# First MLP product: the last pair's P5 with hi beside lo weights, its upper half added through DRAM, and the helper jobs of two stages re-timed

## The chip, the cores and the metric

The kernel runs on one core of one Trainium2 chip. The metric is the device time in microseconds of one execution, the median of several runs. A profiled execution has, beside its time, a span: from its first to its last recorded instruction. Five engines matter: PE (TensorE, with its weight loads as a row of their own, PEld), DVE (VectorE), ACT (ScalarE), POOL (GpSimd, which here issues all accumulating DMAs and a few memsets) and SP (which issues the loads).

## The reference

The input x has 2048 tokens of 640 channels (S, D below), the MLP has 1728 hidden units (F). All is float32.

```python
xn = layernorm(x)                      # no affine part
h  = layernorm(xn)
a  = xn @ dft_hid_re.T ;  b = xn @ dft_hid_im.T
y1 = dft_seq_re @ a - dft_seq_im @ b   # FNet mixing, real part
u  = gelu(h.T @ w1 + b1)               # (D, F): the token-mixing MLP, gelu with tanh
y2 = (u @ w2 + b2).T                   # (S, D)
out = x + y1 + y2
```

## The kernel before

**Number format.** PE takes float32r operands. Each operand is cut into a high part (`high`, an ACT copy to float32r, line 138) and a low part (`low`, a DVE subtraction, line 141). A product is then three matmuls (`three`, lines 149, 150 and 152): high weights by high moving, high weights by low moving, low weights by high moving. The weights are the matrices from DRAM (the "pieces", 128 rows by 512 or 640 columns, cut into blocks of 128), the moving operands are 320 columns of data that stay in SBUF (tiles `shid`, `sup`, `sdown`).

**Stages.** First the products with `dft_seq` (lines 477 and 595, until about 405 us of the span), then four stages of rows: `hid` (8 units, products with `dft_hid`), `up0` and `up1` (7 units each: the first MLP product over the first and the second half of the tokens), `down0` and `down1` (8 units each: the second MLP product over two parts of the hidden units). A unit handles a pair of output row blocks by a Winograd form of Strassen's scheme, with seven products P1, P5, P6, P2, P7, P3, P4 in this order. Each product is a step of the list `steps`; in `up0` and `up1` a step has 4 blocks of 3 matmuls of 128x320.

**The last pair.** The hidden units fill 13 blocks of 128 and a tail of 64 (`TAIL`). Block 13 is paired with block 6 in the last unit, r = 6, of `up0` and of `up1`; on the host its 64 columns are laid out twice. Before the change, the steps P7 and P4 of that unit, whose weights come from block 13 alone, are cut so that the 64 columns of high parts stand beside 64 columns of low parts in one block of weights (`cut_piece` with `tail`, lines 183 to 193): two matmuls per block do, not three. The result has the product with high weights in partitions 0 to 63 of the bank, which DVE adds (line 836), and that with low weights in partitions 64 to 127, which cannot be added across partitions: ACT copies it to a spare tile (line 945) and POOL adds it to the unit's partial result in DRAM by an accumulating DMA (line 934). In `up0` these DMAs wait until the unit's whole result is stored (`end`, line 907), since they add to it.

**Order of the work.** It is written by hand. Turn i (`turn_of`) emits, in this order: `loads[i]` (SP), `reads[i]` (the results of step i-1 out of their PSUM bank, by ACT line 854 or DVE line 841), `sums[i]` (DVE sums of the raw weights, lines 785 and 144), the high cut of step i+2 (ACT), `extras[i]`, `timed[i]`, helper jobs, the low cut of step i+2 (DVE), `behind_lo[i]`, and the matmuls of step i. Every engine takes its instructions in that order. P1, P6, P7 and P4 of a unit accumulate in one PSUM bank (`z`), P5 and P3 in another (`y`), P2 has its own, so that P6, for example, cannot start before ACT has read P1 out of the bank that they share; in the last unit P7 and P4 have a bank `v`.

**Jobs.** The moving operands of the next stage are made by jobs out of a list, at most one per turn: `get` (a load), two normalizations on ACT, and `job0` to `job5` of `moving_of`, of which `job1`, `job2`, `job3` and `job5` are DVE work and are stored as tuples. A turn is "short" when its index is not in `LONG_AT`; a short turn leaves a tuple at the head of the list for later. `None` entries take a turn each.

**Gelu.** In `up1`, unit r's result is gathered by a POOL DMA that adds the part from DRAM (line 911), and two turns of `gelu` (line 916) follow some 14 turns after the unit's start. The first of them is preceded by the load of ACT's table for gelu.

Of the kernel before, what the change touches and what calls it, by code (L numbers as in the profile page):

```python
# [11 lines left out]
AF = mybir.ActivationFunctionType  # L12
ALU = mybir.AluOpType

P = 128
# [6 lines left out]
TAIL = F - NF * P  # L22
# [5 lines left out]
H2 = D // 2  # L28
# [33 lines left out]


LONG_AT = (
    ((0, 1, 3, 6), 7), ((0, 1, 3, 6, 7, 8, 10, 14, 15, 17, 20), 21), ((0, 1, 3, 6), 7), ((0, 1, 3), 7),
)


# [1 line left out]
def fnet_plus_mixer(  # L70
# [30 lines left out]
    nc = tc.nc  # L101
# [8 lines left out]
    one = keep.tile([P, 1], F32, name="one")  # L110
# [32 lines left out]
    def sub(to, a, b):  # L143
        nc.vector.tensor_sub(to, a, b)  # L144
# [19 lines left out]
    steps = []  # L164
    loads, sums, reads, extras, timed, behind_lo = (defaultdict(list) for _ in range(6))
# [103 lines left out]
    def part_of(tag, n):  # L269
# [7 lines left out]
    place = {  # L277
        "v": lambda: pair_at("v"), "ca": lambda: pair_at("ca"), "cb": lambda: pair_at("cb"),
        "x0": part_of("xb", 0), "x1": part_of("xb", 1), "x2": part_of("xb", 2),
    }  # L280
# [486 lines left out]
    def row_steps(stage, nq, load_piece, at, end, bias=(None, None), base=None, earliest=0, each=None, aside={}, tail=False, stacked=()):  # L767

        s0, n = len(steps), nq * P
        raw, banks, held = {}, {}, {}

        def load(*names):
            for name in names:
                raw[name] = raw_slot(n)
                load_piece(raw[name], int(name[1]) - 1, int(name[2]) - 1)  # L780

        def first_sum():
            k = n if n == D else CH
            raw["s"] = raws[k][:, raws[k].shape[1] - 1, :n]
            nc.vector.tensor_add(raw["s"], raw["A21"], raw["A22"])  # L785
            if stacked:

                at = slice(n - P, n)
                nc.vector.tensor_copy(raw["s"][TAIL:, at], raw["A21"][TAIL:, at])

        order = (1, 5, 6, 2, 7, 3, 4)

        early = n < D
        loads_of = {-6: ("A11", "A21", "A22"), -4: ("A12",)} if early else {
            -5: ("A11",), -4: ("A21", "A22"), -1: ("A12",),
        }
        operand = {1: "A11", 5: "s", 6: "A11", 2: "A12", 7: "A21", 3: "A12", 4: "A22"}

        sums_of = {
            -2: (first_sum, lambda: sub(raw["A21"], raw["A11"], raw["A21"])),  # L800
            -1: (lambda: sub(raw["A11"], raw["s"], raw["A11"]),),
            2: (lambda: sub(raw["A12"], raw["A12"], raw["A11"]),),
        }
        bank_of = {1: "z", 6: "z", 7: "z", 4: "z", 5: "y", 3: "y", 2: "w"}
        new_bank = (1, 5, 2)
        if tail:
            bank_of.update({7: "v", 4: "v"})
            new_bank += (7,)
        of_moving = {1: 0, 2: 1, 3: 2, 5: 3, 7: 4, 4: 5, 6: 6}

        goes_to = {1: (0, 0, True), 5: (1, 1, True), 6: (0, 1, True), 2: (0, 0, False), 7: (1, 1, False),
                   3: (0, 1, False), 4: (1, 0, True)}

        def products(i):
            def run(w):
                if i in new_bank:
                    banks[bank_of[i]] = bank()
                for q in range(nq):
                    ks = slice(q * P, (q + 1) * P)
                    m = moving[stage, q]  # L820
                    three(
                        banks[bank_of[i]][:, :H2],
                        (w[0][:, ks], None if w[1] is None or i in stacked and q == nq - 1 else w[1][:, ks]),
                        (m[:, 0, of_moving[i], :], m[:, 1, of_moving[i], :]), i in new_bank and q == 0, q == nq - 1,
                    )
            return run

        def read(i):
            def run():
                if i == 1:  # L830
                    held["c"] = place[at]()
                row, half, fresh = goes_to[i]
                cols = slice(half * H2, (half + 1) * H2)
                c, b = held["c"][:, row, cols], banks[bank_of[i]][:, :H2]
                if tail and i in (7, 4):
                    nc.vector.tensor_add(c[:TAIL], b[:TAIL], c[:TAIL])
                    aside[i](row, half, b)
                elif i in aside:
                    aside[i](row, half, b)
                elif not fresh:  # L840
                    nc.vector.tensor_add(c, b, c)
                elif base and i == 4:

                    for k, queue in enumerate((nc.sync, nc.scalar)):
                        of = slice(k * H2 // 2, (k + 1) * H2 // 2)
                        nc.vector.tensor_add(c[:, of], b[:, of], base()[:, row, cols][:, of])
                        each(c, row, half, True, of, queue)
                    return
                elif base:
                    nc.vector.tensor_add(c, b, base()[:, row, cols])  # L850
                elif bias[row] is not None:
                    nc.scalar.activation(c, b, AF.Identity, bias=bias[row])  # L852
                else:
                    nc.scalar.activation(c, b, AF.Copy)  # L854
                if tail and i == 6:

                    low_row = held["c"][:, 1, :]
                    nc.vector.tensor_add(low_row[:, H2:], b, low_row[:, H2:])
                    nc.scalar.activation(low_row[:, :H2], b, AF.Copy)
                if each:  # L860
                    each(c, row, half, i in (2, 7, 3, 4))
                elif i == 4:
                    end(held["c"])
            return run

        for e, names in loads_of.items():
            loads[max(s0 + e, earliest)].append(lambda names=names: load(*names))
        if s0 == s_hid:


            operand[6] = "s"
            behind_lo[s0 - 2].append(first_sum)
            sums_of = {
                0: (lambda: sub(raw["s"], raw["s"], raw["A11"]),),
                1: (lambda: sub(raw["A21"], raw["A11"], raw["A21"]),),
                2: (lambda: sub(raw["A12"], raw["A12"], raw["s"]),),
            }
        for e, fs in sums_of.items():
            sums[s0 + e].extend(fs)
        for e, i in enumerate(order):  # L880
            steps.append(cut_piece(lambda i=i: raw[operand[i]], n, tail and i in (7, 4), i in stacked) + (products(i),))
            reads[s0 + e + 1].append(read(i))
        return s0

# [13 lines left out]
    def up(stage, r, at):  # L898
# [3 lines left out]
        tail = r == NF2 - 1  # L902
        halves = []
# [29 lines left out]
        def add_to(t, rows, row, half):  # L933
            nc.gpsimd.dma_start(part_up[r][rows, row, half * H2 : (half + 1) * H2], t, accum_op=ALU.add)

        def by_dram(i):
            def run(row, half, b):

                t = place["x1"]()[:, (r + (i == 4)) % 2, i // 7 * H2 : (i // 7 + 1) * H2]
                if not (tail and i in (7, 4)):  # L940
                    nc.scalar.activation(t, b, AF.Copy)
                    add_to(t, slice(P), row, half)
                    return
                t = t[P - TAIL :]
                nc.scalar.activation(t, b[P - TAIL :], AF.Copy)
                if stage == 0:
                    halves.append((row, half, t))
                else:
                    add_to(t, slice(TAIL), row, half)
            return run  # L950

        aside = (2, 7) if stage else ()
        if tail:
            aside += (7, 4)
        s0 = row_steps(
            f"up{stage}", 4, load_piece, at, end, earliest=s_up - 4, aside={i: by_dram(i) for i in aside}, tail=tail,
        )
# [59 lines left out]
    for q in range(4):  # L1017
        get, changes, rest = rows_again(0, q, "v")
# [4 lines left out]
    for r in range(NF2):  # L1023
        up(0, r, ("ca", "cb")[r % 2])
    gets, changes, rests = zip(*(rows_again(1, q, ("v", "x0")[q % 2]) for q in range(4)))
    timed[s_up - 6].append(lambda: jobs.extend([gets[0], None, None] + changes[0]))
    timed[s_up + 2].append(lambda: jobs.extend(
        [gets[1]] + rests[0] + [gets[2]] + changes[1] + rests[1] + [gets[3]] + changes[2] + rests[2]
        + changes[3] + rests[3]
    ))  # L1030
    for r in range(NF2):
        up(1, r, ("x2", "ca", "cb", "v", "x0")[r % 5])
    s_down = len(steps)
# [12 lines left out]
    def do_jobs(n, short=False):  # L1046

        while n > 0 and jobs and not (short and isinstance(jobs[0], tuple)):
            f = jobs.pop(0)
            n -= 1  # L1050
            if f:
                (f[0] if isinstance(f, tuple) else f)()
# [25 lines left out]
    with tc.manual_schedule():  # L1078
        for word in START.split():
            start[word[0]](*map(int, word[1:].split("-")))  # L1080
        for i in range(8, len(steps) + 1):
# [5 lines left out]
            elif i >= s_hid:  # L1087
                k = sum(i >= s for s in (s_up, s_up + 7 * NF2, s_down))
                at, of = LONG_AT[k]
# [43 lines left out]
```

## Time and profile before

| | |
|---|---|
| runs | 876.32, 875.50, 875.51 us: median 875.51 |
| profiled execution | 875.92 us, of which its span 874.2 us |
| PE busy | 869.0 us (99% of the span), 4924 matmuls |
| PE weight loads busy | 793.1 us (91%) |
| DVE busy | 711.7 us (81%) |
| ACT busy | 530.2 us (61%) |
| POOL busy | 126.2 us (14%) |
| granted TensorE clock | 0.999 |
| stage `up0` | 528.9 to 614.3 us of the span |
| stage `up1` | 614.3 to 700.0 us |

Matmuls overlap in the profile, so that the busy time of PE says little on its own: what a matmul costs is the distance from one start to the next, and what is lost is seen where that distance grows. The weight loads stand in a row of their own (PEld), and there the waits show.

### The profile page before, as it was taken

To read this page: it belongs to the slowest core of one execution; us is meant where nothing else is said; L and a number is where in the kernel's file an instruction comes from. 1 tells how busy PE (TensorE), PEld (TensorE's weight loads), DVE (VectorE), ACT (ScalarE), POOL (GpSimd) and SP (SyncE) were. 2 spreads that over 40 slices of the span, in tenths; PEclk is the share of its full clock that TensorE was granted. 3 is DMA by queue.
4 is the path that set the end of the run, shared out by engine and by line. 5 is a ranking of instruction groups with operands and counts; after the bars stand their busy time and mean duration, and the time that the engine had idled before them with its cause. 6 is when DMAs were issued, how large, how long until landed. Compare 5 with 4: busy or idle time off the path is not lost.

```text
span 874.2 us, 13999 instructions
## 1 busy us (share of the span) xinstructions
PE 869.0 (99%) x4924; PEld 793.1 (91%) x4924; DVE 711.7 (81%) x1217; ACT 530.2 (61%) x960; POOL 126.2 (14%) x170
## 2 busy tenths in 40 slices
PE   9999999999999999999999999999999999999998
PEld 6888888888888888889999999999999999999998
DVE  7878878795887978788887787998678978897887
ACT  5746576764556566557565556675577766555553
POOL 0110100101121111222010101000212221111211
PEclk9999999999999999999999999999999999999999
DMA  7771554619385556869666756454678797766786
GB/s 270 231 266 76 194 203 132 242 59 357 54 219 92 163 119 133 208 92 195 168 127 166 156 139 196 162 177 138 142 170 181 169 244 193 190 136 133 151 173 139
DMA packets 86087, 147.64 MB, mean 169 GB/s; under 512 B 8512, under 2 KB 35904, under 8 KB 85760
## 3 DMA queue, kind: packets, MB, share of 16 engines
q1 hardware_dynamic: 64928, 95.80, 34.0%
q0 software_dynamic: 20800, 50.70, 30.6%
q8 instruction: 38, 0.62, 0.3%
q14 instruction: 33, 0.27, 0.1%
q10 hardware_dynamic: 288, 0.25, 0.1%
HBM read 99.96 MB, written 52.00 MB: 174 GB/s over the span
## 4 chain that ended last, share of the span: by engine, by line
PE 94%; DVE 3%; ACT 1%; DMA 1%; issue 1%; DVEq 0%; ACTq 0%
PE psum L149 30%; PE psum L150 30%; PE psum L152 29%; PE psum L477 5%; DVE piece L141 1%; DMA pieces<-y 1%; DVE pieces L144 0%; DMA x<-in_x 0%; ACT piece L138 0%; ACT n L259 0%; ACT x L259 0%; DVE pair L144 0%; DVE st L210 0%; DVE pieces L785 0%; DVE shid L141 0%
## 5 line engine op out<-in xcount | busy, mean ns | idle before, releaser
L141 DVE TENSOR_TENSOR piece<-pieces,piece 128x512 fp32r<-128x512 f32 (+2 forms) x524 | 350.1, 671 | 125.8 <-ACT piece L138 119.1
L138 ACT ACTIVATE piece<-pieces 128x512 fp32r<-128x512 f32 (+3 forms) x508 | 318.1, 627 | 212.0 <-PE psum L152 143.5
L150 PE MATMUL psum<-piece,n 128*128 128x512 f32 x504 | 196.4, 390 | 0.0
L149 PE MATMUL psum<-piece,n 128*128 128x512 f32 x504 | 196.2, 389 | 0.0
L152 PE MATMUL psum<-piece,n 128*128 128x512 f32 x504 | 196.1, 389 | 0.0
L149 PE MATMUL psum<-sup,piece 128*128 128x320 f32 x392 | 121.2, 310 | 0.0
L149 PE MATMUL psum<-sdown,piece 128*128 128x320 f32 x392 | 121.0, 309 | 0.0
L150 PE MATMUL psum<-sup,piece 128*128 128x320 f32 x392 | 120.9, 309 | 0.0
L150 PE MATMUL psum<-sdown,piece 128*128 128x320 f32 x392 | 120.9, 309 | 0.0
L152 PE MATMUL psum<-sup,piece 128*128 128x320 f32 x376 | 116.6, 310 | 0.0
L152 PE MATMUL psum<-sdown,piece 128*128 128x320 f32 x376 | 116.2, 309 | 0.0
L144 DVE TENSOR_TENSOR pieces<-pieces 128x512 f32<-128x512 f32 (+3 forms) x142 | 112.7, 794 | 2.6
L150 PEld LDWEIGHTS psum<-piece,n 128*128 128x128 f32 x504 | 94.6, 188 | 21.0 <-DVE piece L141 1.5
L149 PEld LDWEIGHTS psum<-piece,n 128*128 128x128 f32 x504 | 94.6, 188 | 19.9
L152 PEld LDWEIGHTS psum<-piece,n 128*128 128x128 f32 x504 | 94.6, 188 | 19.3
L152 PE MATMUL psum<-shid,piece 128*128 128x320 f32 x280 | 86.6, 309 | 0.1
L150 PE MATMUL psum<-shid,piece 128*128 128x320 f32 x280 | 86.5, 309 | 0.0
L149 PE MATMUL psum<-shid,piece 128*128 128x320 f32 x280 | 86.5, 309 | 0.0
L854 ACT ACTIVATE pair<-psum 128x320 f32<-128x320 f32 x102 | 44.5, 436 | 54.6 <-PE psum L152 49.8
L149 PEld LDWEIGHTS psum<-sup,piece 128*128 128x128 f32 x392 | 73.6, 188 | 0.6 <-ACT pairs L854 0.3
L149 PEld LDWEIGHTS psum<-sdown,piece 128*128 128x128 f32 x392 | 73.6, 188 | 0.2 <-ACT pair L852 0.2
L150 PEld LDWEIGHTS psum<-sup,piece 128*128 128x128 f32 x392 | 73.6, 188 | 0.0
(106 smaller groups left out, 1115.8 us busy)
## 6 DMA issues: line engine op xcount, KB each, us to landing
pieces<-in_dft_seq SPq DMA_DIRECT2D x128, 256.0 KB, 5.4
pieces<-in_w SPq DMA_DIRECT2D x88, 256.0 KB, 3.7
y<-c POOLq DMA_DIRECT2D x84, 256.0 KB, 6.1
out<-pair POOLq DMA_DIRECT2D x38, 320.0 KB, 5.3
pieces<-y SPq DMA_DIRECT2D x32, 320.0 KB, 3.9
pieces<-in_w SPq DMA_DIRECT2D x32, 192.0 KB, 3.1
out<-in_x SPq DMA_DIRECT2D x16, 320.0 KB, 7.1
up<-pair POOLq DMA_DIRECT2D x8, 640.0 KB, 3.2
```

Of the source, the lines that this page charges most:

```text
L138: nc.scalar.activation(hi, src, AF.Copy)
L141: nc.vector.tensor_sub(lo, src, hi.bitcast(F32))
L144: nc.vector.tensor_sub(to, a, b)
L149: nc.tensor.matmul(psum, wh, mh, start=first, stop=False, skip_group_check=True)
L150: nc.tensor.matmul(psum, wh, ml, start=False, stop=last and wl is None, skip_group_check=True)
L152: nc.tensor.matmul(psum, wl, mh, start=False, stop=last, skip_group_check=True)
L477: nc.tensor.matmul(banks[m, j], channels(k, j)[rows], w[cols], start=n == 0 and k == begin, stop=n == 2 and k == end, skip_group_check=True,)
L854: nc.scalar.activation(c, b, AF.Copy)
```

## The change

- **P5 of the last pair** (r = 6, in `up0` and `up1`) is cut like P7 and P4. Its operand is the sum A21 + A22. `first_sum` now adds only the first 64 columns of each block and sets the other 64 to zero, which the two sums made from it need (one shorter DVE addition and one memset for one full addition). The step has two matmuls per block, not three.
- **P5 gets a bank of its own** ("u"), since its upper half is not to be accumulated into: five banks for that unit, not four, which shifts the turn of the banks behind it. P3 starts the bank "y".
- **C12** (row 0, right half) takes P5's lower partitions straight from bank u by a DVE addition of 64x320 (`behind_lo` of turn s0+4, a new instruction). P5's upper half is copied by ACT and added by two DMAs, to C22 and to C12 (a new ACT copy of 64x320, two new POOL DMAs of 80 KB in each of the two stages).
- **Order in the last pair**: the ACT copies of the upper halves, and the store of the unit after P4, move from `reads` to `extras`, that is behind the high cut of the same turn; so does ACT's copy of C21 (line 859 before). In `up0`, P7's upper half stands first among the DMAs that follow the store, then P5's two, then P4's.
- **Jobs**: in `hid` the turn of index 6 becomes short; in `up0` long turns are now 0, 1 and 3 of every seven (before: 0, 1, 3, 6, 7, 8, 10, 14, 15, 17, 20 of every 21); three `get` entries no longer take a turn of their own.
- **Gelu table**: a small activation of a one-column tile with gelu stands in turn 7 of `up1`, so that the table is loaded there.

On the engines: 8 matmuls with their weight loads fewer (4 in each tail unit), 4 more DVE instructions, 3 more on ACT, 4 more DMAs on POOL; on SP one pair of loads of x stands one load of y later.

```diff
 LONG_AT = (
-    ((0, 1, 3, 6), 7), ((0, 1, 3, 6, 7, 8, 10, 14, 15, 17, 20), 21), ((0, 1, 3, 6), 7), ((0, 1, 3), 7),
+    (tuple(i for i in range(56) if i % 7 in (0, 1, 3, 6) and i != 6), 56), ((0, 1, 3), 7), ((0, 1, 3, 6), 7),
+    ((0, 1, 3), 7),
 )
...
+            if tail:
+                s1, a21, a22 = (raw[a].rearrange("p (q c) -> p q c", c=P) for a in ("s", "A21", "A22"))
+                nc.vector.tensor_add(s1[:, :, :TAIL], a21[:, :, :TAIL], a22[:, :, :TAIL])
+                nc.vector.memset(s1[:, :, TAIL:], 0.0)
+                return
             nc.vector.tensor_add(raw["s"], raw["A21"], raw["A22"])
...
         if tail:
-            bank_of.update({7: "v", 4: "v"})
-            new_bank += (7,)
+            bank_of.update({5: "u", 7: "v", 4: "v"})
+            new_bank += (7, 3)
...
-                if tail and i in (7, 4):
-                    nc.vector.tensor_add(c[:TAIL], b[:TAIL], c[:TAIL])
-                    aside[i](row, half, b)
-                elif i in aside:
+                if tail and i in (5, 7, 4):
+
+                    def upper():
+                        aside[i](row, half, b)
+                        if i == 4:
+                            end(held["c"])
+
+                    extras[s0 + order.index(i) + 1].append(upper)
+                    if i == 5:
+                        nc.scalar.activation(c, b, AF.Copy)
+                    else:
+                        nc.vector.tensor_add(c[:TAIL], b[:TAIL], c[:TAIL])
+                    return
+                if i in aside:
...
-                    nc.scalar.activation(low_row[:, :H2], b, AF.Copy)
+                    extras[s0 + 3].append(lambda: nc.scalar.activation(low_row[:, :H2], b, AF.Copy))
+                    p5 = banks["u"][:TAIL, :H2]
+                    behind_lo[s0 + 4].append(lambda: nc.vector.tensor_add(c[:TAIL], p5, c[:TAIL]))
...
-            steps.append(cut_piece(lambda i=i: raw[operand[i]], n, tail and i in (7, 4), i in stacked) + (products(i),))
+            steps.append(cut_piece(lambda i=i: raw[operand[i]], n, tail and i in (5, 7, 4), i in stacked) + (products(i),))
...
+                for k in (0, 1) if i == 5 else (row,):
+                    if stage == 0:
+                        halves.insert(0 if i == 7 else len(halves), (k, half, t))
+                    else:
+                        add_to(t, slice(TAIL), k, half)
...
-            aside += (7, 4)
+            aside += (5, 7, 4)
...
-        [gets[1]] + rests[0] + [gets[2]] + changes[1] + rests[1] + [gets[3]] + changes[2] + rests[2]
+        [[gets[1]]] + rests[0] + [[gets[2]]] + changes[1] + rests[1] + [[gets[3]]] + changes[2] + rests[2]
...
+    extras[len(steps) + 7].append(lambda: nc.scalar.activation(one, one, AF.Gelu_apprx_tanh))
...
+            if isinstance(f, list):
+                f[0]()
+                continue
```

More of the change, by code (lines that the diff above doesn't have):

```diff
@@ L937, in run @@
             def run(row, half, b):
-                t = place["x1"]()[:, (r + (i == 4)) % 2, i // 7 * H2 : (i // 7 + 1) * H2]
-                if not (tail and i in (7, 4)):
+                at = i in (5, 7)
+                t = place["x1"]()[:, (r + (i in (5, 4))) % 2, at * H2 : (at + 1) * H2]
+                if not (tail and i in (5, 7, 4)):
                     nc.scalar.activation(t, b, AF.Copy)
@@ L945, in run @@
                 nc.scalar.activation(t, b[P - TAIL :], AF.Copy)
[L946 to L949, printed above, removed]
+                for k in (0, 1) if i == 5 else (row,):
[3 more added lines that the diff above has]
+                        add_to(t, slice(TAIL), k, half)
             return run
```

## The prediction

> **What bounds the kernel.** I read the page first, then the waits of the weight loads, then the order of time of single engines around each wait.
>
> ```profile
> PE 869.0 (99%) x4924; PEld 793.1 (91%) x4924; DVE 711.7 (81%) x1217; ACT 530.2 (61%) x960; POOL 126.2 (14%) x170
> ```
> ```profile
> PEld psum L150 <- DVE piece L141: 1.5, 8, 0.3
> ...
> PEld psum L152 <- DVE piece L141: 0.3, 1, 0.3
> PEld psum L149 <- ACT pairs L854: 0.3, 1, 0.3
> PEld psum L149 <- ACT pair L854: 0.3, 1, 0.3
> PEld psum L149 <- ACT pair L852: 0.2, 1, 0.2
> ```
> PE is the bound, and it hardly ever waits: single waits of 0.2 to 0.3 us. So the change can win the pace of the matmuls that it drops and these few waits, and nothing else. The pace is the distance of starts:
>
> ```profile
> 569.83 0.31 PE L152 MATMUL psum<-sup,piece 128*128 128x320 f32 x1
> ...
> 570.42 0.31 PE L149 MATMUL psum<-sup,piece 128*128 128x320 f32 x1
> ```
> Four starts in 0.59 us: 0.147 us for one matmul, not the 0.31 us that its row shows.
>
> **Dropped matmuls.** Four blocks in P5 of each last unit lose one: 4 x 0.147 = 0.59 us in `up0` and 0.59 us in `up1`, 1.17 us together. That is all that PE itself gains; it holds only if the other engines bring everything 0.59 us earlier.
>
> **The job moved in `hid`.**
> ```profile
> 423.48 0.19 PEld L152 LDWEIGHTS psum<-shid,piece 128*128 128x128 f32 x1 [0.34 <-DVE piece L141]
> ```
> ```profile
> 421.35 0.49 DVE L141 TENSOR_TENSOR sup<-pair,sup 128x320 fp32r<-128x320 f32 x1
> 421.87 0.83 DVE L144 TENSOR_TENSOR pair<-pair 128x640 f32<-128x640 f32 x1
> 422.61 0.82 DVE L141 TENSOR_TENSOR piece<-pieces,piece 128x640 fp32r<-128x640 f32 x1
> ```
> PE waits 0.34 us for the low cut at 422.61, ahead of which DVE does a `job1` (421.35 to 422.61, 1.26 us). The short turn 6 moves that job behind the cut, which then is 1.26 us earlier: -0.34. Next late would be the following cut, but that one has the same work ahead of it as before. Later jobs slide by up to three turns and meet again at turn 24. SP's pair of x loads one place later is costed at nothing: its normalization keeps three turns of distance.
>
> **Jobs in `up0`.** Twice a low cut comes late there, in the units r = 1 and 4:
> ```profile
> 543.26 0.38 PE L152 MATMUL psum<-sup,piece 128*128 128x320 f32 x1
> 543.48 0.31 PE L149 MATMUL psum<-sup,piece 128*128 128x320 f32 x1
> ...
> 545.09 0.41 PE L152 MATMUL psum<-sup,piece 128*128 128x320 f32 x1
> 545.34 0.31 PE L149 MATMUL psum<-sup,piece 128*128 128x320 f32 x1
> ```
> Distances 0.22 and 0.25, 0.17 over the pace; r = 4 shows the same form once more, which I count alike: 0.34 in all. Both have a DVE job in turn 6 of a unit, right behind turn 5 with its two sums. With long turns 0, 1 and 3 alone no DVE job stands in turns 4 to 6: -0.34. What was done earlier now lies later: `job1`, `job2` and `job3` of the fourth row come to turns 0, 1 and 3 of the last unit, `job5` to turn 0 of `up1`.
>
> **The last unit of `up0`.** This is where I expect the loss. Before:
> ```profile
> 608.64 0.44 ACT L854 ACTIVATE pair<-psum 128x320 f32<-128x320 f32 x1 [1.01 <-PE psum L152]
> ```
> ```profile
> 609.11 0.49 DVE L858 TENSOR_TENSOR pair<-psum,pair 128x320 f32<-128x320 f32 x1 [1.03 <-ACT pair L854]
> 610.63 0.69 DVE L141 TENSOR_TENSOR piece<-pieces,piece 128x512 fp32r<-128x512 f32 x1 [1.02 <-ACT piece L138]
> 611.24 0.48 DVE L841 TENSOR_TENSOR pair<-psum,pair 128x320 f32<-128x320 f32 x1
> 611.64 0.41 DVE L141 TENSOR_TENSOR piece<-pieces,piece 128x256 fp32r<-128x256 f32 x1
> ...
> 613.68 0.69 DVE L141 TENSOR_TENSOR piece<-pieces,piece 128x512 fp32r<-128x512 f32 x1
> ...
> 615.89 0.48 DVE L836 TENSOR_TENSOR pair<-psum,pair 64x320 f32<-64x320 f32 x1
> ```
> ```profile
> 614.46 0.19 PEld L152 LDWEIGHTS psum<-sup,piece 128*128 128x128 f32 x1
> ```
> From 610.63 to 616.37 DVE is never idle, and the cut at 613.68, of `up1`'s first piece, ends at 614.37, 0.09 us before PE loads it. PE now wants it 0.59 earlier, at 613.87. When does DVE have it? P6 is read 0.59 earlier, so line 858's addition starts at 608.52 and hands over 0.40 later (611.24 to 611.64 for its like), at 608.92. Now comes the moved `job3`, priced by the like job of `down0`:
> ```profile
> 692.03 0.82 DVE L141 TENSOR_TENSOR sdown<-pair,sdown 128x640 fp32r<-128x640 f32 x1
> 692.76 0.49 DVE L144 TENSOR_TENSOR pair<-pair 128x320 f32<-128x320 f32 x1
> 693.16 0.69 DVE L141 TENSOR_TENSOR piece<-pieces,piece 128x512 fp32r<-128x512 f32 x1
> ```
> that is 1.13 us, so that the cut which stood at 610.63 stands at 610.05 (0.58 earlier; without the job ACT's copy of C21 no longer holds up the high cut, and it would be earlier still). From there the old chain of 3.05 us and C12's new addition of 0.40: the cut of 613.68 starts at 613.50, ends at 614.19. PE waits about 0.32 us. The memset beside the shorter first sum lies five turns ahead and is costed at nothing, since DVE idles in between (1.03 us ahead of 609.11 alone); its ends are 0 and 0.7 us, what a full cut takes, and the moved `job1` and `job2` use up most of that idle time.
>
> Then P4 is read at 615.71 (0.18 earlier), and this sets the rest:
> ```profile
> 616.40 0.43 ACT L945 ACTIVATE pairs<-psum 64x320 f32<-64x320 f32 x1 [2.31 <-DVE pair L836]
> ...
> 624.64 0.44 ACT L941 ACTIVATE pairs<-psum 128x320 f32<-128x320 f32 x1 [1.86 <-DMA up<-pairs]
> ```
> ```profile
> 616.89 0.53 POOL L907 DMA_DIRECT2D up<-pair  x1 [12.27 <-ACT pairs L945]
> 620.63 1.73 POOL L934 DMA_DIRECT2D up<-pairs  x2 [3.20 <-ACT pairs L854]
> ```
> P4's upper half follows DVE's addition, then the unit is stored (616.89), its landing lets P7's addition go (620.63), whose landing frees the spare tile that ACT needs to read `up1`'s P7 (624.64, after 1.86 us of waiting), and `up1`'s P4 needs that read. P7's DMA is first before and after, so this whole chain comes just 0.18 us earlier. In between the wait of 0.3 us behind "ACT pairs L854" goes: there ACT read `up1`'s P1 behind P4's upper half and a high cut (the cut now stands ahead of the upper half). And `job5` in `up1`'s turn 0 fits in that room; but all of it is collected again at `up1`'s first P4. So from the last unit of `up0` to there I book -0.18, not -0.59 - 0.3.
>
> On POOL, P5's second addition waits for P7's landing (same bytes), and behind it queue P4's addition, `up1`'s first two and its gather, some 1.7 us later than before; the gelu that uses the gather comes ten turns later, which covers it.
>
> **Gelu's table.**
> ```profile
> 640.48 1.28 ACT L916 ACT_TABLE_LOAD   x1
> 641.78 0.83 ACT L916 ACTIVATE pairs<-pairs,b_sb 128x640 f32<-128x640 f32 x1
> 642.51 0.42 ACT L854 ACTIVATE pair<-psum 128x320 f32<-128x320 f32 x1
> ```
> ```profile
> L130 ACT ACTIVATE one<-one 128x1 f32<-128x1 f32 x1 | 0.2, 203 | 0.0
> ```
> Load and gelu together delay the read at 642.51, for which PE waits 0.3 ("ACT pair L854"). One unit earlier the load stands with a one-column activation in the gelu's place, 0.2 us by the like at the start, so that the read comes at 641.98 in that pattern, 0.53 earlier: no wait, and none at the old place, where the load is gone: -0.3. ScalarE: Activation LUTs, "What ACT_TABLE_LOAD costs", of the Trainium skill gives 1.28 us for the load and 1.38 us more of drain for every switch. The trace has the first, and starts the gelu 0.02 us behind it.
>
> **The last unit of `up1`.**
> ```profile
> 694.56 0.43 ACT L854 ACTIVATE pair<-psum 128x320 f32<-128x320 f32 x1
> ```
> ```profile
> 695.43 0.82 DVE L141 TENSOR_TENSOR sdown<-pair,sdown 128x640 fp32r<-128x640 f32 x1
> 696.54 1.06 DVE L141 TENSOR_TENSOR piece<-pieces,piece 128x512 fp32r<-128x512 f32 x2 [0.29 <-ACT piece L138]
> ```
> Here P6's read at 694.56 follows gelu and a job on ACT, not PE. ACT has P5's upper half more (0.43 for its like at 616.40), of which the read of P5 ahead of it, now sooner, takes back some: the read comes at about 694.8. DVE's addition 0.41 and `job5` 0.73 follow, and P3's low cut starts at 696.36, 0.18 earlier than 696.54, where PE wants it 0.59 earlier. Loss 0.4; C12's addition makes `down0`'s first cut late by another 0.1. The gains are 0.59 and the 0.2 of "ACT pair L852" (the same cause as at `up1`'s start). Net -0.3.
>
> **Sum.** -0.34 - 0.34 - 0.18 - 0.3 - 0.3 = -1.5 us. On the profiled execution (875.92, its span 874.2) that is 874.4 and a span of 872.7. It lies 0.4 above the median of the runs, 875.51, and the sum goes onto the median: **874.0 us**.
>
> **Rivals.**
> 1. *No new waits.* All that is lost above stays won: 1.17 + 0.34 + 0.34 + 0.3 + 0.3 + 0.2 = 2.7 us, 872.8. For it: each new wait is a margin of some tenths in an estimate over 5 us of DVE work. Against it: the DVE and DMA chains above are contiguous. Chance 0.25, with all that lies nearer to it.
> 2. *The landing decides, and is slower.* Store and P7's addition took 616.89 to 624.64, 7.75 us. Four additions now follow the store instead of two, and such DMAs vary:
> ```profile
> up<-pairs POOLq DMA_DIRECT2D x13, 160.0 KB, 5.0
> ...
> up<-pairs POOLq DMA_DIRECT2D x2, 640.0 KB, 8.1
> ```
> Each microsecond more is paid in full by `up1`'s first P4. From 1.5 us more the gain is gone; 8.1 for the store in place of its 3.7 (616.89 to 620.63) would cost 4.4, 878.4: slower. Chance 0.08; up to 1 us more, 875.0, another 0.12.
> 3. *The switch drains.* By the page's rule the read behind the moved load would come 1.38 later, where the rows leave 0.53 - 0.3 = 0.2 of room: 1.2 us on PE, 875.2. The row speaks against it: 0.05.
> My forecast has 0.5.
>
> **Range and chances.** A measurement of this kernel can tell about 0.2% (1.75 us, 873.76) from no change. Rival 1 and a third of the forecast's case lie below that: 0.42; slower by 0.2% is rival 2 at its far end: 0.08; the rest 0.5. The range takes in rival 1's end and a landing 1 us late with some to spare: 872.7 to 875.5.
>
> **What would show it.** PE with 8 matmuls fewer (4916); no wait at 423, 543 and 580; a new wait of 0.3 for a DVE cut right at `up1`'s start; a wait at `up1`'s first P4 behind ACT's read, itself behind "DMA up<-pairs"; the table load in `up1`'s second unit with no PE wait behind it. I am wrong if `up1`'s first P4 does not wait (then rival 1), or if the gather holds up gelu.

## The result, and the profile after

Before: 875.74 us median (875.33 to 876.83, 22 runs). After: 874.63 us (874.36 to 875.02, 22 runs). The ratio is 0.9985, 95% interval 0.9979 to 0.9991: 1.1 us or 0.15% faster, which lies inside what was called no change above, though the interval excludes 1. The profiled execution took 874.65 us with a span of 872.9 (before 875.92 and 874.2), 0.25 us above the 874.4 that the prediction has for a profiled execution.

The page's first row, and the waits of the weight loads (engine, line, waited for: total us, times, longest):

```profile
PE 866.3 (99%) x4916; PEld 791.8 (91%) x4916; DVE 711.5 (82%) x1221; ACT 530.6 (61%) x963; POOL 129.6 (15%) x174
```
```profile
PEld psum L151 <- DVE piece L142: 1.5, 8, 0.3
...
PEld psum L153 <- DVE piece L142: 0.8, 1, 0.8
...
PEld psum L150 <- ACT pairs L964: 0.3, 1, 0.3
```

Eight matmuls are gone, and so are all four single waits of before. Two new ones stand in their place, 0.3 and 0.8 us, each in one of the two last units. The first row, 1.5 us in eight places, is the same in both kernels. (Lines 141, 854, 934 and 945 of before are 142, 870, 952 and 964 of the kernel after.)

Stage by stage, from the first matmul of `hid` (405.35), `up0`, `up1` and `down0` to the last of the kernel, the windows view says (start:end, length, busy time and count of each engine, clock, DMA share, GB/s), first before, then after:

```profile
405.36:528.89 123.53, 123.46 (x842) 123.19 (x841) 99.36 (x144) 68.41 (x114) 14.58 (x17) 1.00 0.71 162
528.89:614.31 85.42, 85.42 (x583) 85.09 (x581) 73.62 (x125) 55.90 (x103) 4.08 (x7) 1.00 0.51 161
614.31:700.03 85.72, 85.71 (x582) 85.06 (x581) 70.36 (x117) 60.61 (x119) 20.01 (x24) 1.00 0.74 168
700.03:870.56 170.53, 170.53 (x1162) 170.04 (x1160) 141.98 (x274) 97.31 (x189) 29.62 (x36) 1.00 0.77 171
```
```profile
405.35:528.68 123.33, 123.33 (x842) 123.20 (x841) 99.22 (x144) 68.44 (x114) 14.58 (x17) 1.00 0.71 162
528.68:613.51 84.83, 84.74 (x579) 84.48 (x577) 73.08 (x125) 55.70 (x104) 4.08 (x7) 1.00 0.52 164
613.51:698.90 85.39, 84.87 (x579) 84.48 (x577) 70.77 (x119) 61.27 (x121) 22.59 (x27) 1.00 0.76 169
698.90:869.31 170.41, 170.41 (x1162) 170.03 (x1160) 142.10 (x275) 97.21 (x189) 30.42 (x37) 1.00 0.77 172
```

`hid` -0.20, `up0` -0.59, `up1` -0.33, `down` -0.12: together -1.24 of the -1.27 us of the span. With no wait at all each of `up0` and `up1` takes 84.48 us (kernel 10 below): `up0` is 0.35 above that, `up1` 0.91.

**The last unit of `up0`.** DVE's order of time, then ACT's copy and the weight load behind it:

```profile
607.96 0.49 DVE L874 TENSOR_TENSOR pair<-psum,pair 128x320 f32<-128x320 f32 x1 [0.32 <-ACT pair L870]
608.37 0.81 DVE L142 TENSOR_TENSOR sup<-pairs,sup 128x640 fp32r<-128x640 f32 x1
609.10 0.48 DVE L145 TENSOR_TENSOR pairs<-pairs 128x320 f32<-128x320 f32 x1
609.50 0.68 DVE L142 TENSOR_TENSOR piece<-pieces,piece 128x512 fp32r<-128x512 f32 x1
...
610.84 0.48 DVE L877 TENSOR_TENSOR pair<-psum,pair 64x320 f32<-64x320 f32 x1
611.24 0.47 DVE L852 TENSOR_TENSOR pair<-psum,pair 64x320 f32<-64x320 f32 x1
```
```profile
611.75 0.43 ACT L964 ACTIVATE pairs<-psum 64x320 f32<-64x320 f32 x1 [0.64 <-DVE pair L852]
```
```profile
612.23 0.19 PEld L150 LDWEIGHTS psum<-sup,piece 128*128 128x128 f32 x1 [0.35 <-ACT pairs L964]
```

The moved `job3` (608.37 and 609.10), C12's new addition (610.84) and P7's addition (611.24) are, with the instructions between them, one chain without a gap. ACT's copy of P7's upper half (611.75) waits for its end, and P4, which shares bank v with P7, waits for ACT: 0.35 us.

**The landing behind it.** POOL and ACT:

```profile
616.16 0.53 POOL L925 DMA_DIRECT2D up<-pair  x1 [12.11 <-ACT pairs L964]
619.90 1.72 POOL L952 DMA_DIRECT2D up<-pairs  x2 [3.20 <-ACT pairs L870]
623.03 3.47 POOL L952 DMA_DIRECT2D up<-pairs  x4 [1.42 <-DMA up<-pairs]
```
```profile
622.83 0.44 ACT L960 ACTIVATE pairs<-psum 128x320 f32<-128x320 f32 x1 [1.13 <-DMA up<-pairs]
```

Store and P7's addition follow each other as before (3.74 us apart), but from that addition to ACT's read of `up1`'s P7 it is now 2.93 us, where it was 4.01. The read ends at 623.27 and P4's matmuls begin at 624.07: 0.8 us of margin, no wait.

**Gelu's table**, in `up1`'s second unit:

```profile
627.00 1.28 ACT L1053 ACT_TABLE_LOAD   x1
628.29 0.20 ACT L1053 ACTIVATE one<-one 128x1 f32<-128x1 f32 x1
628.40 0.42 ACT L870 ACTIVATE pair<-psum 128x320 f32<-128x320 f32 x1
```

The read starts 0.12 us behind the load's end, one small activation between them, and PE does not wait. The 1.38 us of drain that the Trainium skill gives (ScalarE: Activation LUTs, "What ACT_TABLE_LOAD costs") are not in this trace either.

**The last unit of `up1`.** ACT, and then DVE:

```profile
690.27 0.81 ACT L934 ACTIVATE pairs<-pairs,b_sb 128x640 f32<-128x640 f32 x1
690.99 0.42 ACT L850 ACTIVATE pair<-psum 128x320 f32<-128x320 f32 x1
691.31 0.40 ACT L139 ACTIVATE piece<-pieces 128x256 fp32r<-128x256 f32 x1
691.74 0.43 ACT L964 ACTIVATE pairs<-psum 64x320 f32<-64x320 f32 x1
692.20 0.83 ACT L934 ACTIVATE pairs<-pairs,b_sb 128x640 f32<-128x640 f32 x1
692.93 0.72 ACT L139 ACTIVATE sdown<-pair 128x640 fp32r<-128x640 f32 x1
693.68 0.44 ACT L870 ACTIVATE pair<-psum 128x320 f32<-128x320 f32 x1
```
```profile
694.15 0.49 DVE L874 TENSOR_TENSOR pair<-psum,pair 128x320 f32<-128x320 f32 x1 [0.93 <-ACT pair L870]
694.56 0.82 DVE L142 TENSOR_TENSOR sdown<-pair,sdown 128x640 fp32r<-128x640 f32 x1
695.29 1.02 DVE L142 TENSOR_TENSOR piece<-pieces,piece 128x512 fp32r<-128x512 f32 x2
```
```profile
696.03 0.19 PEld L153 LDWEIGHTS psum<-sup,piece 128*128 128x128 f32 x1 [0.78 <-DVE piece L142]
```

P6's last matmul ends at 692.29, and ACT reads the bank at 693.68, behind two gelus of unit r = 4, P5's upper half and a job's high cut. DVE idles 0.93 us for that read, does `job5`, and P3's low cut is 0.78 us late.

### The profile page after: what moved, and what is told of

Read it like the earlier page. It is cut to its first block, busy times and chain, and to the rows that moved or that the text cites. A ratio compares the mean times of both kernels' runs of the same rounds, so it can differ in the third digit from the quotient of the medians.

```text
span 872.9 us, 13995 instructions
## 1 busy us (share of the span) xinstructions
PE 866.3 (99%) x4916; PEld 791.8 (91%) x4916; DVE 711.5 (82%) x1221; ACT 530.6 (61%) x963; POOL 129.6 (15%) x174
## 4 chain that ended last, share of the span: by engine, by line
PE 97%; DVE 1%; ACT 1%; DMA 0%; issue 0%; DVEq 0%
PE psum L150 31%; PE psum L151 31%; PE psum L153 30%; PE psum L478 5%; DMA x<-in_x 0%; DVE piece L142 0%; ACT n L260 0%; ACT x L260 0%; DVE st L211 0%; DVE n L142 0%; DVE sup L142 0%; DVE norm L233 0%; DVE pair L877 0%; DVE r L229 0%; ACT pair L870 0%
```

## The experiments

What each kernel took by stages, from the starts of its first matmuls as in the windows above; "rest" is the span outside of the four stages, where all these kernels are the same:

| kernel | hid | up0 | up1 | down | rest | median us | ratio to before (95%) |
|---|---|---|---|---|---|---|---|
| before | 123.53 | 85.42 | 85.72 | 170.53 | 408.95 | 875.74 | |
| after | 123.32 | 84.83 | 85.39 | 170.41 | 408.92 | 874.63 | 0.9985 (0.9979 to 0.9991) |
| 1 cut only | 123.78 | 84.84 | 85.63 | 170.36 | 408.56 | 874.85 | 0.9991 (0.9982 to 1.0000) |
| 2 re-timing only | 123.45 | 85.07 | 85.40 | 170.53 | 408.59 | 874.53 | 0.9987 (0.9978 to 0.9996) |
| 3 gelus later | 123.45 | 84.83 | 84.98 | 170.45 | 408.19 | 873.53 | 0.9975 (0.9966 to 0.9984) |
| 4 jobs earlier | 123.60 | 84.55 | 85.37 | 170.34 | 408.72 | 874.00 | 0.9982 (0.9973 to 0.9991) |
| 5 = 3 + 4 | 123.20 | 84.54 | 84.97 | 170.34 | 408.04 | 872.97 | 0.9970 (0.9958 to 0.9981) |
| 6 gelus last | 123.20 | 84.54 | 84.48 | 171.48 | 408.03 | 873.53 | 0.9976 (0.9966 to 0.9986) |
| 7 P7 not first | 123.19 | 84.83 | 88.48 | 170.42 | 408.52 | 878.95 | 1.0036 (1.0023 to 1.0050) |
| 8 = 6 + store | 123.65 | 84.54 | 84.48 | 170.35 | 408.21 | 872.92 | 0.9965 (0.9953 to 0.9977) |
| 9 = 8 without the cut | 123.62 | 85.13 | 85.37 | 170.36 | 408.60 | 874.54 | 0.9984 (0.9976 to 0.9993) |
| 10 = 8, other turns | 123.26 | 84.48 | 84.48 | 170.34 | 408.64 | 872.92 | 0.9970 (0.9958 to 0.9981) |
| 11 = 10, x loads later | 124.03 | 84.48 | 84.48 | 170.44 | 408.63 | 872.95 | 0.9970 (0.9959 to 0.9982) |
| 12 = 8 again | 123.34 | 84.55 | 84.48 | 170.35 | 408.53 | 872.54 | 0.9965 (0.9951 to 0.9978) |

Two columns have to be read with care. `hid` and "rest" differ by up to 0.5 and 0.9 us between kernels whose code there is the same; `up0`, `up1` and `down` agree to 0.1 us. So a difference of a few tenths is taken from the stage that was edited, and medians are compared where they differ by more. The stages come from one profiled execution of each kernel. Kernels 1 to 4, 5 to 7, 8 and 9, and 10 to 12 ran together, each group on another chip with the kernel before beside it, and the ratios are to that one. Lines of code that the edits add shift the line numbers of the views by one or two.

**1, the cut alone.** From the kernel after:
```diff
-    (tuple(i for i in range(56) if i % 7 in (0, 1, 3, 6) and i != 6), 56), ((0, 1, 3), 7), ((0, 1, 3, 6), 7), ...
+    ((0, 1, 3, 6), 7), ((0, 1, 3, 6, 7, 8, 10, 14, 15, 17, 20), 21), ((0, 1, 3, 6), 7), ...
-        [[gets[1]]] + rests[0] + [[gets[2]]] + ...
+        [gets[1]] + rests[0] + [gets[2]] + ...
-    extras[len(steps) + 7].append(lambda: nc.scalar.activation(one, one, AF.Gelu_apprx_tanh))
```


> The changed kernel with the old job turns in `hid` and `up0` and without the early gelu activation: only P5's cut, C12's addition from P5's bank and the order of the additions are left. My theory (a job decides): each dropped matmul brings 0.147 us, and what the last units lose again comes from a job that stands in the chain, `job3` in `up0`'s last unit, a gelu and `job5` in `up1`'s. Here `up0`'s last unit has no job, so PE should not wait there (from its start to `up1`'s start 0.59 less than before, where the changed kernel has 0.23 less), nor 0.28 at 617; `up1`'s last unit should still lose 0.8 of its 0.59, and the waits at 423 (0.34), 543 to 582 (0.35) and 642 (0.26) stay. Sum: -1.17 - 0.28 - 0.09 + 0.9 - 0.2 = -0.85 us against before. Rival (the added work decides): C12's addition and P5's upper half fill DVE and ACT without any job; then 0.35 is lost in `up0`'s last unit here too, and the total is -0.5 us.


Measured: 874.85, 0.9 us faster than before (the interval of the ratio just reaches 1), of which the profile has 0.59 in the stages. From the start of `up0`'s last unit to `up1`'s start PE took 0.586 us less, all that four matmuls are worth, and the waits at 617 and 625 were gone. `up1`'s last unit waited 0.77 at the same place as after, with no change of any job. The wait at 423 was 0.60 here, not 0.34. The added work by itself makes nobody late in `up0`; it takes the job beside it.

**2, the re-timing alone.** The inverse: the kernel before, with the three lines above as they are after.


> The kernel before with the new job turns and the early gelu activation, without the cut of P5 (4924 matmuls). My theory: the three gains stand for themselves, -0.21 in `hid`, -0.36 in `up0`, -0.26 at the gelu, and `job3` in `up0`'s last unit costs nothing here, since DVE idled 1.02 us there for ACT's high cut; sum -0.8 us against before, that is the larger half of the change's gain of 1.1 to 1.3, though no arithmetic is saved. Rival (the cut needs the jobs moved, and the move alone only shifts waits): `up0`'s last unit gives back 0.3 or more, sum -0.5 us or less.


Measured: 874.53, 1.2 us faster than before with all 4924 matmuls. `up0` won 0.35 up to its last unit and lost nothing in it; the gelu brought 0.26; `hid` 0.08, since a wait of 0.26 had come in at 454. By stages that is -0.75 (0.35 of the profile's gain lies in "rest"); kernel 1 has -0.59, with 0.25 more in `hid`, where its code is that of before. In `up0` and `up1` alone each of the two brings 0.67. The two parts do not add up: in `up0` -0.58 and -0.35 gave -0.59, for 0.34 is lost where `job3` meets the cut.

**3, the gelus of unit r = 4 later.**
```diff
-            late = 5 if tail else 2 if r >= 4 else 1
+            late = 5 if tail else 4 if r == 4 else 2 if r >= 4 else 1
```


> The changed kernel, with the two gelus of unit r = 4 of `up1` two turns later (turns 3 and 4 of the last unit in place of 1 and 2). My theory: the 0.78 us that PE waits for P3's low cut at 695 come from ACT, which reads P6 1.4 us after PE has ended it, behind P5's upper half, a gelu (0.8) and a job's high cut (0.7); without the two gelus ahead of it the read comes about 1.2 us earlier, DVE's chain with it, and the wait goes down to 0.1 or less: 0.6 to 0.8 us faster than the changed kernel, -1.8 against before. Rival (DVE decides, contiguous from 694.15 to 701.6): the wait goes from P3's cut to P4's bank or to `down0`'s first cut, and at most 0.3 us is won.


Measured: the wait of 0.78 is gone, and one of 0.50 stands at the next consumer, P4's bank. By stages `up1` won 0.41: between the two theories. ACT, and the weight load:
```profile
692.37 0.44 ACT L870 ACTIVATE pair<-psum 128x320 f32<-128x320 f32 x1
...
693.80 0.82 ACT L934 ACTIVATE pairs<-pairs,b_sb 128x640 f32<-128x640 f32 x1
694.52 0.43 ACT L960 ACTIVATE pairs<-psum 128x320 f32<-128x320 f32 x1
694.84 0.42 ACT L139 ACTIVATE piece<-pieces 128x256 fp32r<-128x256 f32 x1
```
```profile
697.02 0.19 PEld L150 LDWEIGHTS psum<-sup,piece 128*128 128x128 f32 x1 [0.50 <-ACT pairs L964]
```
P6's read comes 1.1 us earlier in the unit, but the gelu now stands ahead of P4's high cut (694.84). The median of 873.53, 1.1 below the kernel after, says more than the stages (-0.25 in all); the other 0.7 lie in "rest", and I do not credit them to the edit.

**4, `up0`'s jobs done before its last unit.**
```diff
-    ... ((0, 1, 3), 7), ...
+    ... (tuple(i for i in range(49) if i % 7 in (0, 1, 3) or i in (6, 20, 41)), 49), ...
```


> The changed kernel, with three long turns more in `up0` (turn 6 of its units 0, 2 and 5), which take `job2`, `job5` and `job5`, so that all jobs are done before `up0`'s last unit. My theory: the job in the last unit was what made P4 wait 0.355 us at 611.8 (DVE's chain to P7's addition, which ACT's upper half and with it P4's bank wait for); that wait goes, and the new places cost nothing, since `job3` in turn 6 of unit 2 cost nothing before: 0.35 us faster than the changed kernel, -1.5 to -1.6 against before. Rival (turn 6 is never free): each of the new places costs 0.17 as `job1` did at 543 and 580, and nothing or 0.2 is lost.


Measured: no wait at P4; `up0` 0.28 us shorter than after. Of the three new places one cost 0.07 (`job2` in turn 6, at 543).

**5, both edits.**


> The changed kernel with both edits of the two runs before it: three more long turns in `up0` and unit r = 4's gelus two turns later. My theory (each wait has its own cause, so the gains add): 0.28 from `up0`'s last unit and 0.41 from `up1`'s, 0.7 us faster than the changed kernel, -1.8 to -1.9 against before by stages, apart from the wait at 420 in `hid`, which goes with the landing of a load and was 0.0 to 0.4 us in the runs. Rival (the early part only lets PE run into the later wait, since ACT and DVE in `up1` are late by their own chains): the two together bring no more than the second alone, -2.2 us in the medians as measured there.


Measured: 872.97, 1.7 us below the kernel after; by stages `up0` -0.29 and `up1` -0.42: the gains add.

**6, the gelus behind P7's and P3's reads.** On top of 5:
```diff
-            late = 5 if tail else 4 if r == 4 else 2 if r >= 4 else 1
+            late = 5 if tail else 7 if r == 4 else 2 if r >= 4 else 1
-                timed[e + 6 + late + i].append(lambda i=i: gelu(i))
+                timed[e + 6 + late + (i if r != 4 else 0)].append(lambda i=i: gelu(i))
```


> As the run with both edits, but with both gelus of unit r = 4 in turn 6 of `up1`'s last unit, behind the reads of P7 and P3, where ACT idled 1.7 us. My theory: the 0.5 us that were left at P4's bank (696.5) came from ACT's high cut of P4 behind the first gelu (0.82), which DVE's low cut, C12's and P7's additions and ACT's upper half of P7 follow; without it P4 does not wait: 0.5 us faster than with both edits, some -2.4 against before by stages. Rival (DVE's chain is contiguous on its own, as in the changed kernel from 694.15 on): 0.3 or more of the wait stays, or comes back at `down0`'s start, where ACT now has the gelus ahead of P4's upper half.


Measured: 873.53, 0.6 us slower than kernel 5. `up1` takes 84.48 us, with no wait left, and `down` is 1.14 us longer. The store of that unit, which follows its gelus by two turns, came late. In kernel 5, POOL's store and SP's load of what it stored:
```profile
698.26 0.89 POOL L950 DMA_DIRECT2D up<-pairs  x1
```
```profile
703.27 0.33 SPq L724 DMA_DIRECT2D pairs<-up  x1
703.70 3.77 SPq L989 DMA_DIRECT2D pieces<-in_w  x3
```
and in kernel 6, with DVE's first sum and PE's wait behind it:
```profile
704.90 1.41 POOL L950 DMA_DIRECT2D up<-pairs  x2
```
```profile
712.20 0.33 SPq L724 DMA_DIRECT2D pairs<-up  x1
712.63 2.54 SPq L989 DMA_DIRECT2D pieces<-in_w  x3
```
```profile
721.00 0.69 DVE L792 TENSOR_TENSOR pieces<-pieces 128x512 f32<-128x512 f32 x1 [2.09 <-DMA pieces<-in_w]
```
```profile
723.08 0.19 PEld L154 LDWEIGHTS psum<-sdown,piece 128*128 128x128 f32 x1 [1.14 <-DVE piece L143]
```
The store is 6.6 us later, SP's load, which waits for its landing, 8.9 us, and the weight loads behind that one on SP's queue just as much. Both theories followed the engines alone; neither had the queue.

**7, P7's upper half not first.** From the kernel after:
```diff
-                        halves.insert(0 if i == 7 else len(halves), (k, half, t))
+                        halves.append((k, half, t))
```


> The changed kernel, with the four additions behind `up0`'s last store in the order of the reads: P5's two, P7's, P4's, in place of P7's first. My theory: the landing chain, which I had expected to bind `up1`'s first P4 and which left 0.8 us of margin there (ACT's read of `up1`'s P7 ends at 623.3, P4 starts at 624.07), is real and now binds: P7's addition goes to the same place as P5's second, waits for its landing (some 3.1 us), and lands 3.7 us after that, so that the read comes at about 627.4 instead of 622.83, and PE waits some 3.5 us at P4: 878 us, slower than before. Rival (nobody waits for that landing in earnest, the trace names it only because ACT stood there): no wait at P4, the time of the changed kernel.


Measured: 878.95, slower than before. The profiled execution, 877.21, was the fastest of the five, so the views show 2.6 us of the 4.3 against the kernel after. POOL, ACT's read of `up1`'s P7, and PE:
```profile
619.15 1.72 POOL L952 DMA_DIRECT2D up<-pairs  x2 [2.98 <-DMA up<-pair]
623.39 2.58 POOL L952 DMA_DIRECT2D up<-pairs  x3 [2.52 <-issue]
```
```profile
626.03 0.44 ACT L960 ACTIVATE pairs<-psum 128x320 f32<-128x320 f32 x1 [4.85 <-DMA up<-pairs]
```
```profile
626.51 0.19 PEld L150 LDWEIGHTS psum<-sup,piece 128*128 128x128 f32 x1 [3.08 <-ACT pairs L960]
```
The chain of landings that the prediction followed is real; the order of the four additions is worth more than the rest of the change together.

**8, the store with the gelus.** On top of 6:
```diff
-                timed[e + 8 + late].append(lambda: nc.gpsimd.dma_start(part_up[r], c))
+                timed[e + (8 if r != 4 else 6) + late].append(lambda: nc.gpsimd.dma_start(part_up[r], c))
```


> As the run with unit r = 4's gelus behind P7's and P3's reads, but that unit's store two turns earlier, right behind its gelus, in front of P4's last addition on POOL's queue. My theory: in that run `up1`'s last unit had no wait left, and what it won (0.5 us) was lost again at 721.9 in `down0` (1.14 us) because the store went out at 704.90 instead of 698.26, SP's load of the stored rows waited for its landing until 712, and the four weight loads behind it on SP's queue came late. With the store at about 698.4 the load goes out at 703 again and the wait at 721.9 is gone: 0.5 us faster than the run with both edits, 872.4, the fastest of all. Rival (the later gelus themselves are too late, whatever the store does): 0.5 us or more stays lost in `down0`, 873.0 or slower.


Measured: the store goes out at 699.63, SP's load at 703.92, and the wait in `down0` is gone: by stages 0.5 us better than kernel 5 in `up1`, and the same in `up0` and `down`. The median of 872.92 does not show it (kernel 5: 872.97); the profile lost 0.46 in `hid`, at 454.

**9, the same without the cut**, from the kernel before.


> The run beside it without P5's cut: the same turns of jobs, gelus and store, the early gelu activation, but P5 with all its blocks, its second addition to C22 at once and the old order of the additions (4924 matmuls). My theory: the extra edits bring almost nothing here (nothing waits in the two last units of the kernel before but 0.28 at 617, 0.03 at 697, 0.19 at 703), so it stands with the run of the first re-timing, 874.5; the difference to the run beside it is then what the cut is worth when every chain is clear of jobs: 1.17 for the matmuls and up to 0.6 for the waits that the later upper halves remove, 1.2 to 1.8 us. Rival (the re-timing would have brought its gain without the cut): 873.5 or less here.


Measured: 874.54, as kernel 2: the extra edits bring nothing without the cut. Against kernel 8 the cut is worth 1.6 us by the medians and 1.48 by `up0` and `up1`: 1.17 for the matmuls and some 0.3 for the wait at 617. That one goes because the upper halves are copied later, which belongs to the cut here and was not run by itself.

**10, other long turns.** On top of 8:
```diff
+    ((0, 1, 2, 3, 4), 7), ((0, 1, 2, 3, 4), 7), ((0, 1, 3, 6), 7), ((0, 1, 3), 7),
```


> As the run with the gelus behind P7's and P3's reads and the store with them, but in `hid` and `up0` the long turns are 0, 1, 2, 3 and 4 of every unit: no DVE job stands in turns 5 and 6, where a unit's two sums and its third one lie. My theory (a job waits for nothing, it makes PE wait only where DVE's chain to the next low cut is full): the waits at 454 (0.08 to 0.46 us in the runs, where the change lets `job1` slide into turn 6) and at 543 (0.07) go, and turns 2 and 4, which were short before, cost nothing, since DVE has one sum or one addition there: 0.15 to 0.5 us faster than the run beside it, 872.4 to 872.8. Rival (turns 2 and 4 were short for a reason): new waits of 0.1 to 0.3 for a low cut in many units of both stages, several microseconds in all.


Measured: no wait at 454 and 543, and none in turns 2 and 4. By stages it is the shortest of all (0.16 below kernel 12), but its median, 872.92 beside 872.54, does not say so. Mechanism shown, gain not.

**11, `hid`'s first x loads three turns later.** On top of 10:
```diff
-        ... js=[get, None, None] + changes + rest ...
+        ... js=[None] * 3 * (q == 0) + [get, None, None] + changes + rest ...
```


> As the run beside it, with `hid`'s first pair of x loads three turns later. My theory: the wait at 420 in `hid`, which was 0.0, 0.04, 0.22, 0.40 and 0.43 us in profiles of kernels with the same turns there, goes with the landing of the third `pieces` load of the second unit (5.2 to 6.3 us, 3.5 to 4 for the two loads after it); the x loads are issued 4 to 7 us ahead of it on the same queue. With these out of the way it lands 1 us earlier and PE does not wait: up to 0.3 us faster in the median, and no slip at 420 in the profile. Rival (POOL's stores of y, 7 to 8 us each, hold that load up): its landing stays at 5 to 6 us and the median is the same.


Measured: the third load landed in 3.3 us, not 5.9, and nothing waits at 420. But SP's queue, freed of the x loads, sent the next weight load 4.7 us earlier (401.86 for 406.57), a store of y beside it took 7.8 us to land (5.0 in kernel 10), and ACT's read of `hid`'s first product began (409.95) as that store landed (409.88): PE waited 0.83. I take the store for the cause; the profile does not name it.
```profile
410.44 0.19 PEld L149 LDWEIGHTS psum<-shid,piece 128*128 128x128 f32 x1 [0.83 <-ACT pair L869]
```
This profile was the slowest of its six runs; the median is that of its neighbour. Inconclusive on the time.

**12, kernel 8 again.**


> The same kernel as the run with the gelus behind P7's and P3's reads and the store with them (872.92 in its first measurement), beside the two kernels that are built on it. My theory: 872.9 again, 1.7 us faster than the changed kernel; by stages from `up0`'s start on it is 0.5 us faster than the run with both edits, and the medians did not show that because `hid` lost it (0.46 at 454 in its profile). Rival (the gelus' last move is worth nothing): 873.0 or more.


Measured: 872.54; from `hid` on no two matmul starts are more than 0.15 us further apart than the pace. Kernel 8 in its two sets (872.92 and 872.54, ratio 0.9965) is ahead of both kernels of the case: 3.0 us faster than before by the medians, some 1.9 faster than the change as it was made. The four stages have 2.2 and 2.5 of the 3.0, and 0.9 and 1.2 of the 1.9 (kernels 8 and 12); the rest of it lies in "rest", and I do not count it here either. Against kernels 5 and 10 its lead is not settled.

## Why the prediction was right, and where only by balance

The time (874.63 for 874.0) is inside the range, and the case that was called likeliest came in: most of what the cut and the waits would give is lost again in the two last units. By its own steps, on the profiled execution:

| step | predicted | measured |
|---|---|---|
| job moved in `hid` | -0.34 | -0.20 |
| jobs in `up0` | -0.34 | -0.36 |
| last unit of `up0`, to `up1`'s second unit | -0.18 | -0.59 |
| gelu's table | -0.3 | -0.26 |
| last unit of `up1` and `down0`'s start | -0.3 | +0.10 |

- **Matmuls**: 0.147 us each; kernel 1 has the 0.586 of a last unit to the hundredth.
- **`hid`** was mis-sized: I said that the jobs that slide cost nothing. One of them, `job1`, slides into turn 20, a turn 6 of its unit again, and costs 0.08 at 454 (0 to 0.46 in other profiles). And the wait at 423 is not DVE's alone: DVE's first sum waits there for the landing of a load, and the first cut behind it was 0.34 and 0.60 us late in the two profiles with the old turns, 0.0 to 0.43 in ten with the new ones. With that spread one pair of profiles does not settle the -0.20.
- **`up0`'s last unit**: the DVE chain was right, 0.35 of wait for 0.32. It struck one consumer earlier than I said, at P4's bank through ACT's upper half, not at `up1`'s first cut; I had not followed the bank that P7 and P4 share.
- **The landing** is the step that failed. I took over 4.0 us from P7's addition to ACT's read; it was 2.93, so the predicted wait at `up1`'s first P4 did not come, and 0.4 us more were kept. What differs is SP. Two weight loads of 256 KB start at 619.98 before, 0.65 us ahead of the addition, and 1.30 ahead after:
```profile
619.98 0.90 SPq L900 DMA_DIRECT2D pieces<-in_w  x2
```
```profile
618.60 0.90 SPq L918 DMA_DIRECT2D pieces<-in_w  x2
```
In ten kernels these loads start 1.3 us ahead, and the addition lands in 2.7 to 3.1 us; in three (before, 2 and 9) they start 0.65 ahead, and it takes 3.6 to 3.9. But these three are also the kernels without the cut, and POOL differs there too: it sends a third addition, of 160 KB, 1.9 us behind P7's,
```profile
622.55 0.89 POOL L934 DMA_DIRECT2D up<-pairs  x1 [0.20 <-issue]
```
where with the cut it waits for P7's landing (623.03 above). Kernel 7 speaks against POOL as the cause: there two more additions follow P7's within 1.1 us, its loads start 1.1 and 1.5 us ahead, and it lands in 2.6. Moving the loads alone was not tried, so the cause stays open. The condition that I had given for being wrong, no wait at that P4, was met, and yet rival 1 did not follow: its 2.7 us need both last units free of waits, and kernel 7 shows that only 0.8 us of margin kept the landing off the path.
- **`up1`'s last unit** was mis-sized by the same amount the other way. I let P5's read, now sooner, take back 0.2 of the 0.43 of its upper half. But that read stands behind a gelu (690.27 to 690.99) and came only 0.16 sooner in the unit, and the steps from it to P6's read, 1.99 us before, took 2.69. P6's read was 0.54 late for my 0.24, and the wait 0.78 for 0.4, with 0.1 more at P4's bank.
- **Rival 2** would have been true with the additions in another order (kernel 7: +3.2 us); **rival 3** is out.

So two errors of 0.4 us cancelled. The sum was right by its shape, a chain of margins that are nearly used up, and by luck in its size.

## What to carry to other kernels

Where one engine is busy 99% of the time, dropping its work pays only as far as every chain that feeds it is clear: here the cut brought 0.7 us in its two stages by itself and 1.5 once jobs, two gelus and a store had been moved out of its way. Follow such a step to every consumer of the late engine, the next bank as well as the next cut, and to the queues: moving an activation moved a store, the store held a load, and the load held the weights. A landing time is not a constant of a transfer; take a range over the transfers beside it.

## What was not expected of the hardware

- The same accumulating DMA of 80 KB, P7's in `up0`, landed in 2.6 to 3.9 us, and the same load of `pieces` in `hid`, the one of kernel 11, in 4.9 to 6.3 us (3.3 in kernel 11), in profiles of nearly the same kernels.
- The start of `hid` lay between 404.88 and 405.36 us, and the time from the last matmul to the end of the span was 3.15 to 3.18 us in five profiles, 3.32 in one and 3.57 to 3.59 in eight, with the same code in both places. No run here tells what sets either. Together they move a time by as much as most of the edits did. It need not be chance from run to run: all ten runs of kernel 3 lie within 0.4 us, and all below the fastest of the kernel after, though its stages give 0.25 of that alone.
